# Moving the skip-and-inverse-transform stage of a fused FFN and long-convolution backward kernel from the middle of the program to its output tiles

## The chip, the cores and the metric

One core of a Trainium2 chip. The metric is the device time of one execution in microseconds (us). The kernel before took 2041.97 us (median of 6 runs, 2040.7 to 2049.8). All times below are of runs in the fast state. TensorE is called PE, VectorE DVE, ScalarE ACT, GpSimd POOL and SyncE SP, as in the profile.

## The reference, cut to what matters

The reference runs the forward pass and the gradients of one block with two branches that share a layernorm:

```python
def _f(x, ...):                         # L, D, F, N = 2048, 576, 4608, 128, bf16
    xn = _layernorm(x)
    return x + _A_ref(xn, ...) + _B_ref(xn, ...)
def _A_ref(u, ...):                     # long convolution
    K = einsum("dn,dnl,dn->dl", C, exp(dt*A*l), dt*B).real     # length-2048 kernel per channel
    y = irfft(rfft(u) * rfft(K))[:L]
    return y + u * Dskip
def _B_ref(x, Wg, Wu, Wd):              # gated FFN
    g = x @ Wg;  g = g * (g > 0)
    return (g * (x @ Wu)) @ Wd
out, vjp = jax.vjp(_f, ...);  return out, *vjp(grad_out)
```

There are thirteen outputs: the forward output, the gradient of x, eight small parameter gradients and three FFN weight gradients. Only the first two are touched by the main part of the change. Each needs a sum of three terms: the layernormed input (or the gradient) times `Dskip`, an inverse transform of the convolution, and the FFN's rows, which are accumulated over twelve chunks of F. The forward output also has x added; for the gradient of x the sum then goes through the layernorm's backward pass.

## The kernel before: the parts that matter

Two generators write the program. The FFN generator goes through 12 chunks of 384 columns; within each chunk through four groups of rows. The convolution generator is pulled beside it, so that PE always has one while the other waits. Both yield estimated us, and a pacing constant decides how much convolution is pulled per us of FFN:

```python
PACE = 0.95
W1, W2, W3 = 56.0, 400.0, 91.0
    for us in ffn.gen(ln, final):
        if us == "last": ...            # what is left of the convolution is drained here
        ft += us
        while s4_open and stt < PACE * (ft - start):
            r = next(sgen, None)
            ...
def gen(self):                          # the convolution
    ...                                 # transforms, parameters
    yield from self.p1(0)
    yield from self.both(self.p2(0, pools), 0.8 * W2, self.p1(1), W1)
    yield from self.both(self.p2(1, pools), 0.8 * W2, self.p3(0), W3)
    yield from self.p3(1)
    yield from self.grads()
```

`W3` sets how the work of `p3(0)` (products and back transforms of the first half of the 576 columns) is spread over `p2(1)` (kernel powers, second half). The end of `p3`, for each half, is the base stage:

```python
            bp = self.pool(c, f"p3_d{hf}", 2)
            for n2 in range(ST):                                   # 16 tiles of 128 rows
                S3 = self.dft(bp, self.s3_dram, n2)
                Ct = bp.tile([P, 2, 2, DH], BF16, name="bC2")
                nc.sync.dma_start(Ct[:], self.C[2][hf][:, n2])
                xt = bp.tile([P, 3, DH], BF16, name="xt")
                nc.sync.dma_start(xt[:, 0, :], g.x_v[:, n2, cols])
                nc.sync.dma_start(xt[:, 1:3, :], g.xg_dram[:, n2, :, cols])
                o = bp.tile([P, 2, DH], F32, name="base")
                v.tensor_tensor(o[:], xt[:, 1:3, :], dsk..., op=ALU.mult)              # L726
                v.tensor_tensor(o[:, 0, :], o[:, 0, :], xt[:, 0, :], op=ALU.add)
                for i in range(2):
                    v.tensor_tensor(o[:, i, :], o[:, i, :], self.back2(S3, Ct, i), op=ALU.add)
                nc.sync.dma_start(self.base_dram[:, n2, :, cols], o[:])                # L730
```

The f32 result waits in DRAM until the last FFN chunk, in which each output tile is finished once its FFN rows are complete:

```python
def final_tile(g, s4, pool, small, t):
    base = pool.tile([P, 2, D], F32, name="f_base")
    nc.sync.dma_start(base[:], s4.base_dram[:, t])
    acc = pool.tile([P, 2, D], BF16, name="f_acc")
    nc.sync.dma_start(acc[:], g.acc_dram[:, t])
    xg = pool.tile([P, 2, D], BF16, name="f_xg")
    nc.sync.dma_start(xg[:], g.xg_dram[:, t])
    ...
    nc.vector.tensor_tensor(o[:, 0, :], base[:, 0, :], acc[:, 0, :], op=ALU.add)     # L989
    ...                                                                              # layernorm backward
```

Of the kernel before, what the change touches and what calls it, by code (L numbers as in the profile page):

```python
# [14 lines left out]
P = 128  # L15
# [6 lines left out]
ST = 16  # L22
# [11 lines left out]
PACE = 0.95  # L34
W1, W2, W3 = 56.0, 400.0, 91.0
# [139 lines left out]
class Ffn:  # L175
# [121 lines left out]
    def rows(self, c, i):  # L297
        g, nc = self.g, self.g.nc
        for n in range(i, min(i + 3, 4 + NK)):
            if (c, n) not in self.R:  # L300
                t = self.dp.tile([P, ST, 144], BF16, name="rows")
                src = g.gq_dram[n] if n < 4 else g.xs_dram[n - 4]
                nc.sync.dma_start(t[:, :, 0:144 if n < 4 else min(P, D - (n - 4) * P)], src[:])
                self.R[(c, n)] = t
# [52 lines left out]
    def gen(self, ln, final):  # L357
        lu = FTC - 1
        ready = []
        for c in range(NFC):  # L360
# [10 lines left out]
            else:  # L371
# [20 lines left out]
                yield 3.0  # L392
                for ft in range(3, FTC):
# [59 lines left out]
class S4:  # L453
    def __init__(self, g, aps, outs, Dskip):
# [8 lines left out]
        self.dk_dram = two("dk_dram", [P, ST, DH])  # L463
# [3 lines left out]
        self.base_dram = d("base_dram", [P, ST, 2, D], F32)  # L467
# [177 lines left out]
    def p1(self, hf):  # L645
# [28 lines left out]
        with ExitStack() as c:  # L674
            bp = self.pool(c, f"p1_c{hf}", 3)
            for n2 in range(ST):
                S3 = self.dft(bp, self.s3_dram, n2)
                Ct = bp.tile([P, 1, 2, DH], BF16, name="bC1")
                nc.sync.dma_start(Ct[:], self.C[1][hf][:, n2])
                o = bp.tile([P, DH], BF16, name="dk_o")  # L680
                g.bal.copy(o[:], self.back2(S3, Ct, 0), DH)
                nc.sync.dma_start(self.dk_dram[hf][:, n2, :], o[:])
                yield 0.3


    def p3(self, hf):
# [26 lines left out]
        with ExitStack() as c:  # L713
            cp = self.pool(c, f"p3_c{hf}", 1)
            dsk = cp.tile([P, DH], BF16, name="dsk")
            nc.sync.dma_start(dsk[:], self.Dskip[cols].rearrange("(o d) -> o d", o=1).to_broadcast([P, DH]))
            bp = self.pool(c, f"p3_d{hf}", 2)
            for n2 in range(ST):
                S3 = self.dft(bp, self.s3_dram, n2)
                Ct = bp.tile([P, 2, 2, DH], BF16, name="bC2")  # L720
                nc.sync.dma_start(Ct[:], self.C[2][hf][:, n2])
                xt = bp.tile([P, 3, DH], BF16, name="xt")
                nc.sync.dma_start(xt[:, 0, :], g.x_v[:, n2, cols])
                nc.sync.dma_start(xt[:, 1:3, :], g.xg_dram[:, n2, :, cols])
                o = bp.tile([P, 2, DH], F32, name="base")
                v.tensor_tensor(o[:], xt[:, 1:3, :], dsk[:].unsqueeze(1).to_broadcast([P, 2, DH]), op=ALU.mult)  # L726
                v.tensor_tensor(o[:, 0, :], o[:, 0, :], xt[:, 0, :], op=ALU.add)
                for i in range(2):
                    v.tensor_tensor(o[:, i, :], o[:, i, :], self.back2(S3, Ct, i), op=ALU.add)
                nc.sync.dma_start(self.base_dram[:, n2, :, cols], o[:])  # L730
                bal.add(d=1.8)
                yield 1.8
# [16 lines left out]
    def p2(self, hf, pools):  # L749
# [4 lines left out]
        for d0 in range(hf * DH, (hf + 1) * DH, P):  # L754
# [5 lines left out]
            for s0 in range(0, dsz, SC):  # L760
# [4 lines left out]
                nc.sync.dma_start(dkr[:], self.dk_dram[hf][:, :, dd0 - hf * DH:dd0 - hf * DH + SC])  # L765
# [212 lines left out]
def final_tile(g, s4, pool, small, t):  # L978
    nc, bal = g.nc, g.bal
    inv_d = 1.0 / D  # L980
    base = pool.tile([P, 2, D], F32, name="f_base")
    nc.sync.dma_start(base[:], s4.base_dram[:, t])
    acc = pool.tile([P, 2, D], BF16, name="f_acc")
    nc.sync.dma_start(acc[:], g.acc_dram[:, t])
    xg = pool.tile([P, 2, D], BF16, name="f_xg")
    nc.sync.dma_start(xg[:], g.xg_dram[:, t])
# [19 lines left out]
def kernel(  # L1006
# [67 lines left out]
    fin = []  # L1074

    def final(t):
        if not fin:
            fin.extend(fctx.enter_context(tc.tile_pool(name=n, bufs=3, reuse_waits="tile")) for n in ("fin", "fin_small"))
        final_tile(g, s4, fin[0], fin[1], t)
# [5 lines left out]
    for us in ffn.gen(ln, final):  # L1085
        if us == "last":
            if s4_open:
                s4_open = False
                for r in sgen:
                    stt += r  # L1090
            continue
# [43 lines left out]
```

## Time and profile before

| | before |
|---|---|
| median, range (6 runs) | 2041.97 us, 2040.7 to 2049.8 |
| span of the profiled run | 2047.9 us |
| PE busy over the span | 1860.5 us, 91% |
| usual start spacings of all matmuls added up ("work") | 1700 us |
| the rest of the time from the first FFN unit ("lost") | 330 us |

The prediction shows the busy shares, the stretches and the waits. Two more lines of the page count here: what the DMA engines moved, in packets by size, and the share of their time that SyncE's queue took.

```profile
DMA packets 390368, 372.86 MB, mean 182 GB/s; under 512 B 196042, under 2 KB 314058, under 8 KB 389898
...
q1 hardware_dynamic: 339402, 288.02, 46.8%
```

Half of all packets are below 512 B. Two of the change's parts are aimed at these.

"Work" and "lost" are used throughout, as the prediction defines them (its "finer measure than busy"). The measure is stricter than PE busy: a matmul of 288 columns is recorded as 286 ns although such matmuls start 122 ns apart, so the records also cover some gaps, and 1860.5 us of busy hold 1700 us of work.

Lost time is not all waiting. The trace also records the clock granted to PE; the page's row PEclk and the column behind the busy times show it. In some short stretches it is 0.5, and there 288-column matmuls start 240 ns apart in place of 122. Its mean is 0.978 over the 2047.9 us, so at most 45 us of the lost time (an estimate from this mean) are matmuls at a slower clock.

### The profile page before, as it was taken

How to read it: one execution, taken by the hardware profiler on the slowest of the kernel's cores; microseconds unless marked ns; L12 is line 12 of the kernel's file. 1: busy time of each engine (PE TensorE's matmuls, PEld its weight loads, DVE VectorE, ACT ScalarE, POOL GpSimd, SP SyncE). 2: the span in 40 equal slices, each digit the busy share in tenths (PEclk: the TensorE clock that was granted, in tenths of full speed). 3: DMA queues.
4: the chain of work that ended last, by engine and by line, in shares of the span. 5: the costliest groups of instructions: out<-in, count | busy, mean ns of one | idle time of the engine just before them, and what ended most of it. 6: DMA issues, size and time to landing. Idle time of an engine off the chain costs nothing.

```text
span 2047.9 us, 44531 instructions
## 1 busy us (share of the span) xinstructions
PE 1860.5 (91%) x16919; PEld 1256.9 (61%) x16919; DVE 1464.3 (72%) x3633; ACT 1467.7 (72%) x3244; POOL 255.9 (12%) x321
## 2 busy tenths in 40 slices
PE   6988897989999999999999999999999889788977
PEld 3665565646756766765766766666676565456545
DVE  7454772799888787897789779779877356555573
ACT  3664673799979879888878978867878645453562
POOL 5120010001101101101101101101111100110110
PEclk8999999999999999999999999999999999999999
DMA  9556888755845748747755765687765786977797
GB/s 332 199 167 180 252 219 219 185 156 131 194 136 131 180 133 184 148 132 174 190 153 117 167 154 132 149 210 197 166 138 127 184 227 205 263 194 173 213 264 206
DMA packets 390368, 372.86 MB, mean 182 GB/s; under 512 B 196042, under 2 KB 314058, under 8 KB 389898
## 3 DMA queue, kind: packets, MB, share of 16 engines
q1 hardware_dynamic: 339402, 288.02, 46.8%
q0 software_dynamic: 29248, 63.72, 19.6%
q10 hardware_dynamic: 21504, 18.29, 3.0%
q8 instruction: 132, 2.16, 0.4%
q14 instruction: 82, 0.67, 0.1%
HBM read 220.74 MB, written 149.20 MB: 181 GB/s over the span
## 4 chain that ended last, share of the span: by engine, by line
PE 37%; ACT 23%; DVE 16%; DMA 16%; issue 5%; SPq 1%; POOL 0%; ACTq 0%; DVEq 0%; POOLq 0%
PE ps_mm L248 9%; PE ps_mm L332 8%; PE ps_mm L290 7%; ACT osx L66 3%; ACT YT L66 2%; PE ps_mm L319 2%; PE ps_s L611 2%; PE pt L272 2%; PE ps_s L869 2%; PE ps_s L612 1%; DMA base_dram<-base 1%; ACT ysn L811 1%; ACT ycs L813 1%; ACT hN L66 1%; DMA A_k<-fA 1%
## 5 line engine op out<-in xcount | busy, mean ns | idle before, releaser
L66 ACT CAST osx<-ps_mm 128x288 bf16<-128x288 f32 x716 | 279.5, 442 | 51.3 <-PE ps_mm L290 49.9
L295 POOL DMA_DIRECT2D acc_dram<-osx x176 | 152.8, 868 | 1221.5 <-ACT osx L66 865.7
L290 PE MATMUL ps_mm<-wgT,dgT 128*128 128x288 bf16 x1152 | 217.7, 288 | 4.9 <-ACT osx L66 1.5
L290 PE MATMUL ps_mm<-wuT,duT 128*128 128x288 bf16 x1152 | 215.7, 289 | 0.0
L248 PE MATMUL ps_mm<-xT,wg 128*128 128x512 bf16 x720 | 205.0, 389 | 6.5 <-ACT osx L66 3.4
L332 PEld LDWEIGHTS <-rows 128*128 128x128 bf16 x1536 | 147.7, 98 | 93.6 <-issue 4.4
L290 PE MATMUL ps_mm<-wd,hT 128*128 128x288 bf16 x1152 | 192.8, 291 | 5.1 <-ACT rg L253 1.6
L248 PE MATMUL ps_mm<-xT,wu 128*128 128x512 bf16 x720 | 194.4, 389 | 0.0
L248 PE MATMUL ps_mm<-gT,wdT 128*128 128x512 bf16 x720 | 189.5, 384 | 0.2 <-DVE upm L255 0.2
L255 DVE SCALAR_TENSOR_TENSOR upm<-rg,ps_mm 128x512 bf16<-128x512 bf16 x144 | 98.3, 683 | 113.0 <-PE ps_mm L248 75.4
L319 PE MATMUL ps_mm<-rows,hN 128*128 128x144 bf16 x2304 | 162.6, 230 | 14.9 <-DMA rows<-gq_dram 14.7
L319 PEld LDWEIGHTS <-hN 128*128 128x128 bf16 x2304 | 153.3, 100 | 18.6 <-DMA rows<-gq_dram 10.8
L66 ACT COPY YT<-ps_s 128x1024 bf16<-128x1024 bf16 x139 | 142.7, 1027 | 16.0 <-PE ps_s L869 14.8
L332 PE MATMUL ps_mm<-dgN,rows 128*128 128x384 bf16 x768 | 148.8, 329 | 2.7 <-DMA rows<-xs_dram 2.6
L885 DVE TENSOR_TENSOR pr<-X,ps_s 128x256 f32<-128x256 f32 x288 | 109.1, 415 | 51.5 <-PE ps_s L881 51.1
L66 ACT CAST dhb<-ps_mm 128x512 bf16<-128x512 f32 x144 | 86.1, 598 | 78.1 <-PE ps_mm L248 77.0
L332 PE MATMUL ps_mm<-duN,rows 128*128 128x384 bf16 x768 | 140.9, 326 | 0.0
L290 PEld LDWEIGHTS <-dgT 128*128 128x128 bf16 x1152 | 111.5, 98 | 37.0 <-issue 9.9
L290 PEld LDWEIGHTS <-hT 128*128 128x128 bf16 x1152 | 108.6, 99 | 37.8 <-issue 9.7
L290 PEld LDWEIGHTS <-duT 128*128 128x128 bf16 x1152 | 112.7, 99 | 29.7 <-issue 1.1
L248 PEld LDWEIGHTS <-wdT 128*128 128x128 bf16 x720 | 70.5, 99 | 79.7 <-issue 7.3
L248 PEld LDWEIGHTS <-wu 128*128 128x128 bf16 x720 | 70.4, 100 | 73.9 <-issue 9.5
(244 smaller groups left out, 4175.2 us busy)
## 6 DMA issues: line engine op xcount, KB each, us to landing
acc_dram<-osx POOLq DMA_DIRECT2D x192, 288.0 KB, 4.6
gT<-gT_dram SPq DMA_DIRECT2D x44, 640.0 KB, 5.9
xT<-xT_dram SPq DMA_DIRECT2D x44, 640.0 KB, 5.6
rows<-gq_dram SPq DMA_DIRECT2D x48, 576.0 KB, 4.7
rows<-xs_dram SPq DMA_DIRECT2D x48, 512.0 KB, 5.1
A_ug<-fA SPq DMA_DIRECT2D x32, 288.0 KB, 2.8
out_dram<-obw SPq DMA_DIRECT2D x96, 96.0 KB, 2.8
b_ug<-A_ug SPq DMA_DIRECT2D x32, 288.0 KB, 3.5
```

The source lines that it names most:

```text
L66: self.nc.scalar.copy(out, in_)
L248: nc.tensor.matmul(ps[:], lhsT=w[:, k, fs], rhs=rhs[:, k, :], start=(k == 0), stop=(k == NK - 1))
L255: nc.vector.scalar_tensor_tensor(upm[:], rg[:], 0.0, ps_u[:], op0=ALU.is_gt, op1=ALU.mult)
L272: nc.tensor.transpose(out=pt[:, j, :], in_=src[:, j * P:(j + 1) * P], identity=g.ident_bf[:])
L290: nc.tensor.matmul(ps[:, :DH], lhsT=lt[:, js], rhs=rh, start=(i == 0), stop=(i == len(mms) - 1))
L295: nc.gpsimd.dma_start(g.acc_dram[:, t, :, :], o[:], accum_op=ALU.add)
L319: nc.tensor.matmul(ps[:, (ft - f) * 144:(ft - f + 1) * 144], lhsT=self.hN[:, st, ft * P:(ft + 1) * P], rhs=gq[:, st, :], start=(st == 0), ...
L332: nc.tensor.matmul(ps[:, :Fc], lhsT=xs[:, st, 0:P], rhs=src[:, st, :], start=(st == 0), stop=(st == ST - 1))
L611: nc.tensor.matmul(ps[:, :DH], lhsT=CC[:], rhs=src[:, o, :], start=True, stop=False)
L612: nc.tensor.matmul(ps[:, :DH], lhsT=sm[:], rhs=src[:, other, :], start=False, stop=True)
L869: nc.tensor.transpose(out=tb[:, i * P:(i + 1) * P], in_=Y[:, ri, dl, :], identity=g.ident_bf[:])
L885: nc.vector.tensor_tensor(pr[:], X[:, dx:dx + DG, r0:r0 + 2].rearrange("p d r a -> p d (r a)").unsqueeze(2).to_broadcast(sh), psg[:, 0:DG ...
```

## The change

The intent is to spare the round trip of `base_dram` and to put the base's DVE and PE work where those engines have holes, in the last chunk. Beside this, two DMA layouts get longer runs, and the pacing constants follow the shorter convolution.

```diff
-PACE = 0.95
-W1, W2, W3 = 56.0, 400.0, 91.0
+PACE = 0.9
+W1, W2, W3 = 56.0, 400.0, 62.0
@@ rows of x and grad for the weight gradients: packed in the tile
-                nc.sync.dma_start(t[:, :, 0:144 if n < 4 else min(P, D - (n - 4) * P)], src[:])
+                w = 144 if n < 4 else min(P, D - (n - 4) * P)
+                v = t[:].rearrange("p t d -> p (t d)")[:, 0:ST * w].rearrange("p (t d) -> p t d", d=w)
+                nc.sync.dma_start(v, src[:])
@@ dk: collected in SBUF, stored once in its reader's order
-        self.dk_dram = two("dk_dram", [P, ST, DH])
+        self.dk_dram = two("dk_dram", [P, DH // SC, ST, SC])
... (the loop writes into one tile; one store behind it; the reader takes one run)
@@ the base stage leaves p3
-            for n2 in range(ST):
-                ... (the base stage above, with its store)
+    def base(self, pools, got):
+        S3, Ct, xt, xg = got
+        o = three.tile([P, 2, D], F32, name="f_base")
+        v.tensor_tensor(o[:], xg[:], dsk..., op=ALU.mult)                              # L743
+        for i in range(2):
+            for hf in range(2):
+                for ri in range(2):
+                    nc.tensor.matmul(ps, lhsT=S3[:, ri, :], rhs=Ct[:, hf, i, ri, :], ...)
+                if i == 0:
+                    nc.tensor.matmul(ps, lhsT=g.ident_bf[:], rhs=xt[:, cols], ...)     # + x
+                v.tensor_tensor(o[:, i, cols], o[:, i, cols], ps, op=ALU.add)          # L752
@@ and is made in the last chunk: fetched four tiles ahead, computed two tiles ahead
+    def final(t):
+        fetch_to(t + 4 + 1)
+        for n in range(t, min(t + 2 + 1, ST)):
+            if n not in bases:
+                bases[n] = s4.base(fin, got[n])
+        base, xg = bases[t]
+        final_tile(g, base, xg, fin[2], fin[2], t)
@@ the first three bases come early in the last chunk
+                if c == NFC - 1:
+                    yield "early"
```

More of the change, by code (lines that the diff above doesn't have):

```diff
@@ L302, in rows @@
                 src = g.gq_dram[n] if n < 4 else g.xs_dram[n - 4]
-                nc.sync.dma_start(t[:, :, 0:144 if n < 4 else min(P, D - (n - 4) * P)], src[:])
-                self.R[(c, n)] = t
+                w = 144 if n < 4 else min(P, D - (n - 4) * P)
+                v = t[:].rearrange("p t d -> p (t d)")[:, 0:ST * w].rearrange("p (t d) -> p t d", d=w)
+                nc.sync.dma_start(v, src[:])
+                self.R[(c, n)] = v
         return self.R[(c, i)]
@@ L466, in __init__ @@
         self.R_dram = d("R_dram", [P, 4, D], F32)
-        self.base_dram = d("base_dram", [P, ST, 2, D], F32)
     def pool(self, ctx, name, bufs):
@@ L675, in p1 @@
             bp = self.pool(c, f"p1_c{hf}", 3)
+            dk = self.pool(c, f"p1_d{hf}", 1).tile([P, DH // SC, ST, SC], BF16, name="dk")
+            sp = self.pool(c, f"p1_e{hf}", 2)
             for n2 in range(ST):
-                S3 = self.dft(bp, self.s3_dram, n2)
+                S3 = self.dft(sp, self.s3_dram, n2)
                 Ct = bp.tile([P, 1, 2, DH], BF16, name="bC1")
                 nc.sync.dma_start(Ct[:], self.C[1][hf][:, n2])
-                o = bp.tile([P, DH], BF16, name="dk_o")
-                g.bal.copy(o[:], self.back2(S3, Ct, 0), DH)
-                nc.sync.dma_start(self.dk_dram[hf][:, n2, :], o[:])
+                g.bal.copy(dk[:, :, n2, :], self.back2(S3, Ct, 0).rearrange("p (g d) -> p g d", d=SC), DH)
                 yield 0.3
+            nc.sync.dma_start(self.dk_dram[hf][:], dk[:])
     def p3(self, hf):
@@ L712, in p3 @@
                 yield 1.5
-        with ExitStack() as c:
-            cp = self.pool(c, f"p3_c{hf}", 1)
-            dsk = cp.tile([P, DH], BF16, name="dsk")
-            nc.sync.dma_start(dsk[:], self.Dskip[cols].rearrange("(o d) -> o d", o=1).to_broadcast([P, DH]))
-            bp = self.pool(c, f"p3_d{hf}", 2)
-            for n2 in range(ST):
-                S3 = self.dft(bp, self.s3_dram, n2)
-                Ct = bp.tile([P, 2, 2, DH], BF16, name="bC2")
-                nc.sync.dma_start(Ct[:], self.C[2][hf][:, n2])
-                xt = bp.tile([P, 3, DH], BF16, name="xt")
-                nc.sync.dma_start(xt[:, 0, :], g.x_v[:, n2, cols])
-                nc.sync.dma_start(xt[:, 1:3, :], g.xg_dram[:, n2, :, cols])
-                o = bp.tile([P, 2, DH], F32, name="base")
-                v.tensor_tensor(o[:], xt[:, 1:3, :], dsk[:].unsqueeze(1).to_broadcast([P, 2, DH]), op=ALU.mult)
-                v.tensor_tensor(o[:, 0, :], o[:, 0, :], xt[:, 0, :], op=ALU.add)
-                for i in range(2):
-                    v.tensor_tensor(o[:, i, :], o[:, i, :], self.back2(S3, Ct, i), op=ALU.add)
-                nc.sync.dma_start(self.base_dram[:, n2, :, cols], o[:])
-                bal.add(d=1.8)
-                yield 1.8
@@ new lines, in fetch @@
+    def fetch(self, pools, t):
+        g, nc = self.g, self.g.nc
+        one, ahead, three, xgp = pools
+        if t == 0:
+            self.dsk = one.tile([P, D], BF16, name="dsk")
+            nc.sync.dma_start(self.dsk[:], self.Dskip.rearrange("(o d) -> o d", o=1).to_broadcast([P, D]))
+        S3 = ahead.tile([P, 2, P], BF16, name="S3")
+        nc.sync.dma_start(S3[:], self.s3_dram[:, t])
+        Ct = ahead.tile([P, 2, 2, 2, DH], BF16, name="bC2")
+        for hf in range(2):
+            nc.sync.dma_start(Ct[:, hf], self.C[2][hf][:, t])
+        xt = ahead.tile([P, D], BF16, name="xt")
+        nc.sync.dma_start(xt[:], g.x_v[:, t, :])
+        xg = xgp.tile([P, 2, D], BF16, name="f_xg")
+        nc.sync.dma_start(xg[:], g.xg_dram[:, t])
+        return S3, Ct, xt, xg
@@ new lines, in base @@
+    def base(self, pools, got):
+        g, nc, bal = self.g, self.g.nc, self.g.bal
+        v = nc.vector
+        one, ahead, three, xgp = pools
+        S3, Ct, xt, xg = got
+        o = three.tile([P, 2, D], F32, name="f_base")
+        v.tensor_tensor(o[:], xg[:], self.dsk[:].unsqueeze(1).to_broadcast([P, 2, D]), op=ALU.mult)
+        for i in range(2):
+            for hf in range(2):
+                cols = slice(hf * DH, (hf + 1) * DH)
+                ps = self.ps()[:, :DH]
+                for ri in range(2):
+                    nc.tensor.matmul(ps, lhsT=S3[:, ri, :], rhs=Ct[:, hf, i, ri, :], start=(ri == 0), stop=(ri == 1 and i == 1))
+                if i == 0:
+                    nc.tensor.matmul(ps, lhsT=g.ident_bf[:], rhs=xt[:, cols], start=False, stop=True)
+                v.tensor_tensor(o[:, i, cols], o[:, i, cols], ps, op=ALU.add)
+        bal.add(d=2.7)
+        return o, xg
@@ L764, in p2 @@
                 dkr = parp.tile([P, ST, SC], BF16, name="dkr")
-                nc.sync.dma_start(dkr[:], self.dk_dram[hf][:, :, dd0 - hf * DH:dd0 - hf * DH + SC])
+                nc.sync.dma_start(dkr[:], self.dk_dram[hf][:, (dd0 - hf * DH) // SC])
                 dkc = parp.tile([P, SC, 2, ST], BF16, name="dkc")
@@ L974, in gen, with final_tile @@
         yield from self.grads()
-def final_tile(g, s4, pool, small, t):
+def final_tile(g, base, xg, pool, small, t):
     nc, bal = g.nc, g.bal
     inv_d = 1.0 / D
-    base = pool.tile([P, 2, D], F32, name="f_base")
-    nc.sync.dma_start(base[:], s4.base_dram[:, t])
     acc = pool.tile([P, 2, D], BF16, name="f_acc")
     nc.sync.dma_start(acc[:], g.acc_dram[:, t])
-    xg = pool.tile([P, 2, D], BF16, name="f_xg")
-    nc.sync.dma_start(xg[:], g.xg_dram[:, t])
     xn, gt = xg[:, 0, :], xg[:, 1, :]
@@ L1074, with fetch_to @@
     fin = []
-    def final(t):
-        if not fin:
-            fin.extend(fctx.enter_context(tc.tile_pool(name=n, bufs=3, reuse_waits="tile")) for n in ("fin", "fin_small"))
-        final_tile(g, s4, fin[0], fin[1], t)
+    bases = {}
+    got = {}
+    def fetch_to(n):
+        if not fin:
+            fin.extend(fctx.enter_context(tc.tile_pool(name=f"fin_{i}", bufs=n, reuse_waits="tile")) for i, n in enumerate((1, 3, 3, 6)))
+        for m in range(min(n, ST)):
+            if m not in got:
+                got[m] = s4.fetch(fin, m)
+    def final(t):
+        fetch_to(t + 4 + 1)
[4 more added lines that the diff above has]
+        final_tile(g, base, xg, fin[2], fin[2], t)
     sgen = s4.gen()
@@ L1085 @@
     for us in ffn.gen(ln, final):
-        if us == "last":
+        if us == "last" or us == "early":
             if s4_open:
@@ L1090 @@
                     stt += r
+            if us == "early":
+                fetch_to(4 + 1)
+                for n in range(3):
+                    bases[n] = s4.base(fin, got[n])
             continue
```

## The prediction

> **What bounds the kernel now.** I read the page's busy shares first, then the row of 40 slices, then a table by stretches that I cut myself, then the waits and the chain in the two worst stretches.
>
> ```profile
> PE 1860.5 (91%) x16919; PEld 1256.9 (61%) x16919; DVE 1464.3 (72%) x3633; ACT 1467.7 (72%) x3244; POOL 255.9 (12%) x321
> ...
> PE   6988897989999999999999999999999889788977
> ...
> DVE  7454772799888787897789779779877356555573
> ...
> DMA  9556888755845748747755765687765786977797
> ```
>
> TensorE is busy 91% of the span, and in the middle slices nothing is to be had from anybody else. But the last nine slices (from about 1590 us) have sevens and eights on PE while VectorE falls to five and six tenths and the DMA row climbs to nine. So the end is not bound by an engine; something there waits for transfers. The stretches (columns: us, then busy us of PE, PEld, DVE, ACT, POOL, then the granted clock, the DMA share and GB/s):
>
> ```profile
> 460.00:1322.00 862.00, 824.68 (x8172) 571.67 (x8171) 721.85 (x1721) 742.62 (x1625) 110.69 (x115) 0.99 0.64 152
> 1322.00:1484.00 162.00, 150.80 (x1488) 105.10 (x1487) 135.14 (x301) 124.94 (x261) 19.76 (x21) 0.99 0.75 192
> ...
> 1741.00:1803.00 62.00, 49.43 (x347) 31.57 (x347) 37.68 (x82) 26.86 (x60) 6.90 (x8) 0.94 0.95 262
> ...
> 1914.00:1986.00 72.00, 57.54 (x393) 35.56 (x392) 51.13 (x113) 44.92 (x103) 9.46 (x11) 0.95 0.93 249
> 1986.00:2047.90 61.90, 49.16 (x449) 36.35 (x447) 25.95 (x55) 23.86 (x54) 3.45 (x4) 0.94 0.79 217
> ```
>
> 1322 to 1484 holds the base stage of the first half of the columns (it multiplies xn and grad by Dskip, adds two back transforms and stores f32 rows), 1741 to 1803 that of the second half. There the DMA engines are 95% busy, PE only 80%. The waits in that stretch name the loads:
>
> ```profile
> DVE base L726 <- DMA xt<-xg_dram: 13.5, 9, 2.6
> PE ps_s L641 <- DMA bC<-C_ydu: 9.9, 4, 3.9
> ...
> DVE base L726 <- DMA xt<-in_A_u_dram: 5.2, 1, 5.2
> ```
>
> 1914 to 1986 is the last chunk, in which the output tiles are finished while the FFN still runs. VectorE, in order, stands before the accumulated rows, ScalarE stands behind VectorE, and PE then waits for an eviction (hN) on ScalarE:
>
> ```profile
> DVE f_o L989 <- DMA f_acc<-acc_dram: 16.0, 5, 4.6
> ACT f_acc L994 <- DVE f_base L992: 12.3, 5, 3.9
> ...
> PE pt L272 <- ACT hN L66: 9.0, 6, 3.9
> ```
>
> A finer measure than busy: the usual distance between starts of matmuls in the trace is 216, 163, 122 and 63 ns for 512, 384, 288 and 144 columns. Adding these up over the matmuls of a stretch gives its pure work; the rest of the stretch is lost. Lost share: 10% in 460 to 1322 (778 us of work in 862), 12% in 1322 to 1487 (145 in 165), 20% in 1587 to 1741, 32% in 1741 to 1803 (44.3 in 65, as its last gap reaches beyond it), 27% in 1914 to 1986 (52.4 in 72), 23% in 1986 to 2048.
>
> **What the Trainium skill says.** "TensorE: Matmul & The Clock Gate", Back-to-back issue gap: N/2.4 + 2.5 ns when warm. For 288 columns that is 122.5 ns; the trace has 122. "VectorE: DVE Perf Modes", the perf-mode tier table and the errata section: tensor_tensor with an fp32 or a PSUM operand runs at one element per cycle, (N+151)/0.96 ns. For 576 that is 757 ns; the trace has 756 (the multiply by Dskip). I use it for the one new shape, 1152 elements: 1357 ns, an estimate. "DMA: Bandwidth & Descriptors", Specifications: below 512 B a transfer is off line rate. The packets of this trace agree only in part: 256 B took 18.5 ns, 4608 B 218 ns, so small ones cost more per byte, but not wildly.
>
> **The change, part by part.**
>
> 1. The two base stages leave the middle. They hold 128 matmuls of 288 columns (15.6 us of PE) and 128 DVE instructions. Second half: 44.3 us of work less 7.8 leaves 36.5; at a lost share of 10 to 20% that needs 40 to 46 us instead of 62, so 16 to 22 us come free. First half: 145 less 7 is 138, at 10% lost 152 instead of 165, so 13 us. Together about -32.
>
> 2. base_dram goes. It was written (32 x 288 KB) and read (16 x 576 KB): 18.9 MB. xg is read once in place of twice in these stages: 4.7 MB. Total 372.9 to about 349 MB. This is mostly the cause of part 1, so I add nothing for it again.
>
> 3. The rows of xs are packed tightly in the tile, so each partition is one run of 4096 B (2048 B for the last block) and not 16 of 256 B (128 B): 122,880 packets become some 7,700. The dk tensor gets the layout of its reader: 36,864 packets of 64 B become 2,304 of 1024 B. Packets under 512 B fall from 196 thousand to about 36 thousand. The mean packet times give the DMA engines 48 us (rows) and 18 us (dk) of their time back, each. But PE waited for rows from xs only 2.6 us on its matmuls in the whole run, and the transfers are already hidden. -3.
>
> 4. dk collects in SBUF and is stored once. In 307 to 358 us (first half, where nothing else of the convolution runs) 17.8 us are lost, and the loads of C_dk stood behind stores in SyncE's order. I give it -6; the second half is hidden behind the K computation, -1. The one late store (1.1 MB, some 6 us by the kk load of the same size) may take part of this back.
>
> 5. PACE 0.95 to 0.9 and W3 91 to 62 spread the shorter work over the same FFN time; by the yields of the generators it still ends at 1266 against 1263 of 1396 virtual us. No drain at the end. 0.
>
> 6. The last chunk takes the bases over. PE: 128 matmuls, and 32 new ones that add x through the identity, 160 x 122.5 ns = 19.6 us. DVE: 16 multiplies of 1152 elements (1.36 us) and 64 adds from PSUM (0.447 us, the row of L729), 50 us. The order of instructions of the changed kernel tells where: four multiplies and about 12 adds before the second group of rows (the place of 1914 us), 8 and 34 up to the last gated activation (1986 us), the rest behind.
>  - 1866 to 1914: VectorE has room (20 of 48 us). PE pays 3.7 us. +4.
>  - 1914 to 1986: PE work 52.4 + 8 tiles x 10 x 0.1225 = 62 us. DVE busy 51.1 + 8 x 1.36 + 34 x 0.447 - 2.3 (five evictions that the order now has on ScalarE) = 75 us. That is above the stretch itself: VectorE becomes the bound. At its utilisation in the middle, 722 of 862 us or 84%, it needs 89 us; at its best slice, 96%, 78 us. I choose 85, so +13. The waits for the accumulated rows shrink, since multiplies stand before them in VectorE's order, but what VectorE gains there it spends on the bases.
>  - 1986 to the end: 4 or 5 tiles, 6 us of PE between the down-weight matmuls, with two PSUM buffers that VectorE has to free. +4.
>  Together +21.
>
> Sum: -32 - 3 - 7 + 21 = -21. From 2042: about 2020. The loads are now issued four tiles ahead, which may save more of the 19.5 us lost in 1914 to 1986 than I allowed; I put the middle at 2015.
>
> **The rivals.**
>  - A: VectorE becomes the bound of the last chunk and gives back half of the gain (my choice). For: the 75 us above. Against: nothing, except that the order could let PE run ahead. 2005 to 2025.
>  - B: The end is set by transfers alone, and removing base_dram frees it: last chunk no longer than before. For: DMA share 0.93 there, and the 16 us wait of DVE is a DMA. Against: the changed kernel fetches more per tile there, not less: C 576 KB, x 144, the transform 64, in place of 576 KB of base; and the wait is for acc, which stays. This makes 1990 to 2000, over 2%.
>  - C: With prefetches queued before it, the load of acc lands later, VectorE waits as before and the bases come on top. For: SyncE issues in order, and 1072 KB of fetches per tile go ahead of an acc of 288 KB. Against: the first five tiles are fetched before 1914. The last chunk is 40 us longer: 2035 to 2045.
>  - D: The descriptors matter more than their waits show (DMA share 0.64 in the middle falls, all landings get quicker): another -10 to -20. Against: PE loses 10% in the middle, and its waits there are for evictions, not transfers.
>
> **Range and chances.** A has most weight, B and D together a fifth, C a tenth. Predicted 2015 us, 8 in 10 between 1990 and 2036. Faster by over 2% (below 2001 us) needs B or D: 0.22. Within 2%: 0.74. Slower by over 2%: 0.04, an unforeseen stall of PE behind the two PSUM buffers.
>
> **What would show it.** Steps 1 and 2: about 349 MB, no base_dram, the time from the start of the second kernel transform (L600 with kk) to the start of the last chunk shorter by some 20 us. Step 3: some 36 thousand packets under 512 B, DMA share in the middle down from 0.64, PE busy there unchanged. Step 4: fewer than 12 us lost in the dk stage. Step 6: from the first final tile to the last gated activation, 80 to 90 us in place of 72, with VectorE over 85% busy. I am wrong if that stretch is not longer, if VectorE still has tens of us of waits for f_acc there, or if the middle (before the second base stage) shortens by more than 25 us.

## The result, and the profile after

The changed kernel took 1993.26 us (median of 8 runs, 1988.73 to 1996.18) against 2043.39 us for the kernel before (16 runs, 2039.64 to 2049.8, of the same rounds). The ratio is 0.9751, 95% interval 0.9737 to 0.9765. Ratios here and below are the mean time of one kernel's fast runs over the mean of the other's fast runs of the same rounds, so not quite the ratio of the medians. The outputs are correct. The result is inside the predicted range (1990 to 2036) but 22 us below its middle and 3 us above its lower end, and it is faster by 2.5%, an outcome that the prediction gave only 0.22.

The page of the changed kernel: busy us and instructions of each engine, then the rows of 40 slices of PE, DVE and DMA, then the packets and SyncE's queue.

```profile
PE 1842.9 (93%) x16951; PEld 1256.1 (63%) x16951; DVE 1452.8 (73%) x3593; ACT 1461.0 (73%) x3236; POOL 256.2 (13%) x321
...
PE   6989897889999999999999999999999979989988
...
DVE  7454862699878877888778878879888615664795
...
DMA  9556888656746735844854655655654577776895
...
DMA packets 214125, 348.19 MB, mean 175 GB/s; under 512 B 34266, under 2 KB 131930, under 8 KB 213402
...
q1 hardware_dynamic: 163162, 263.37, 40.6%
```

Bytes and small packets are as worked out (about 349 MB, some 36 thousand). In the row of slices the sevens of PE near the end are gone except one, and DVE now has a seven and a nine in the 38th and 39th slice: the bases. The stretches that answer to those of the prediction: the middle, the time of the old first base stage, the time of the old second one, the last chunk's gated groups, and the end.

```profile
460.00:1301.00 841.00, 807.79 (x8047) 563.85 (x8046) 691.06 (x1616) 718.04 (x1562) 111.34 (x116) 1.00 0.60 150
1301.00:1465.00 164.00, 158.45 (x1680) 114.08 (x1676) 137.56 (x325) 139.19 (x301) 19.55 (x20) 1.00 0.58 152
1745.00:1801.00 56.00, 47.52 (x460) 37.00 (x459) 37.59 (x152) 29.59 (x76) 6.93 (x8) 0.97 0.69 159
1850.00:1925.00 75.00, 68.99 (x508) 45.15 (x507) 66.68 (x141) 50.83 (x114) 10.37 (x12) 1.00 0.91 249
1925.00:1991.30 66.30, 54.82 (x474) 39.95 (x473) 41.27 (x85) 23.92 (x54) 3.45 (x4) 0.89 0.63 184
```

The reader is to compare the fourth line with the prediction's line for 1914 to 1986. The stretch is 75 us in place of 72, although PE is busy 11 us more in it and DVE 16 us more. The waits of that stretch tell why (us in total, times, longest):

```profile
DVE upm L255 <- PE ps_mm L248: 5.8, 1, 5.8
ACT f_acc L1012 <- DVE f_base L1010: 5.6, 5, 3.4
DVE f_o L1007 <- DMA f_acc<-acc_dram: 4.6, 1, 4.6
```

DVE's wait for the accumulated rows was 16.0 us and is 4.6; the wait of PE for the eviction `hN`, 9.0 us before, is no longer among the waits that matter. Multiplies and adds of the bases now stand in DVE's order where it used to wait.

Where the time went, by stretches of the FFN (wall us, with lost us in brackets; "chunk 5b" is the third group of rows of chunk 5). The old first base stage lies in the second row, the old second one in the third. "Base move" is the experiment e4 below:

| stretch | before | base move | changed | PACE 0.86 | loads ahead |
|---|---|---|---|---|---|
| first unit to chunk 5b | 923.0 (151.5) | 920.3 (150.0) | 900.6 (137.0) | 892.0 (131.3) | 922.9 (152.4) |
| chunk 5b to chunk 9 | 566.3 (63.6) | 551.7 (52.6) | 547.0 (51.5) | 540.9 (49.8) | 565.0 (62.4) |
| chunk 9 to chunk 11 | 358.7 (72.7) | 320.0 (47.2) | 335.6 (53.6) | 326.9 (39.8) | 342.1 (56.2) |
| chunk 11 to the end | 182.1 (42.1) | 191.6 (32.1) | 190.4 (30.7) | 218.4 (56.4) | 190.3 (50.4) |
| sum | 2030.1 (330) | 1983.6 (282) | 1973.6 (273) | 1978.2 (277) | 2020.3 (321) |

(Some 18 us ahead of the first unit are the same in all.) The work, wall less lost, is about 1700 us in every kernel. So all of the gain is lost time that PE no longer loses: 330 to 273 us. Up to some 13 of these 57 us are the granted clock: its mean rose from 0.978 to 0.984, which by the estimate above leaves 32 us in place of 45. No run tells whether the clock rose only because PE waited less.

The profile of the kernel before is of one of its longer runs (2049.8 us), so the table's total difference is some 6 us larger than that of the medians.

### The profile page after: what moved, and what is told of

Its sections match the earlier page's. It is cut to its first block, busy times and chain, and to the rows that moved or that the text cites. A ratio compares the mean times of both kernels' runs of the same rounds, so it can differ in the third digit from the quotient of the medians.

```text
span 1991.3 us, 44207 instructions
## 1 busy us (share of the span) xinstructions
PE 1842.9 (93%) x16951; PEld 1256.1 (63%) x16951; DVE 1452.8 (73%) x3593; ACT 1461.0 (73%) x3236; POOL 256.2 (13%) x321
## 4 chain that ended last, share of the span: by engine, by line
PE 40%; ACT 24%; DVE 19%; DMA 10%; issue 5%; SPq 0%; POOL 0%; ACTq 0%; DVEq 0%; POOLq 0%
PE ps_mm L248 10%; PE ps_mm L334 8%; PE ps_mm L290 7%; ACT osx L66 4%; PE ps_mm L321 2%; ACT YT L66 2%; PE ps_s L614 2%; ACT hN L66 2%; PE ps_s L891 2%; PE ps_s L615 2%; ACT dgN L66 1%; ACT ysn L833 1%; ACT duN L66 1%; DVE pr L907 1%; PE ps_mm L348 1%
## 5 line engine op out<-in xcount | busy, mean ns | idle before, releaser
L248 PE MATMUL ps_mm<-gT,wdT 128*128 128x512 bf16 x720 | 184.9, 379 | 0.0
```

The lines of the kernel that those rows point to most:

```text
L248: nc.tensor.matmul(ps[:], lhsT=w[:, k, fs], rhs=rhs[:, k, :], start=(k == 0), stop=(k == NK - 1))
```

## The experiments

The theory after the result: the gain is the base move, which costs little at the end because the last chunk was full of holes; the layouts give nothing; the pacing gives some, because a thinner mix of convolution and FFN loses less. The rival theory: the smaller packets relieve the DMA queues everywhere, and the base move gives only the 11 us that the prediction netted for it. Each experiment gave the reference's outputs. They ran in four sessions (e1 to e4, e5 to e8, e10 to e12, e13), each on a chip of its own and beside its own runs of the kernel before. The changed kernel was timed apart from them, so that its ratio and an experiment's are compared across sessions.

### e1_rows: the packed rows alone, in the kernel before

```diff
-                nc.sync.dma_start(t[:, :, 0:144 if n < 4 else min(P, D - (n - 4) * P)], src[:])
+                (the packed view of the change)
```

> The kernel before with the packed rows tiles alone (4096 B runs in place of 256 B). If transfers of rows were hidden as the prediction said: -3 us (ratio 0.998 to 1.000), though packets under 512 B fall by 123 thousand. If the small packets slowed everything by their use of the DMA engines (rival D): -10 us or more, ratio 0.995 or below, and the stretch of the second base stage, which was bound by transfers, gets shorter too.

Measured: 2048.16 us (22 runs) against 2046.81 (35 runs), ratio 1.0009, interval 0.9994 to 1.0025. Packets under 512 B fell from 196 thousand to 73 thousand, and the DMA share in the middle from 0.64 to 0.62. The time did not move. 123 thousand small packets fewer are worth nothing here, which fits the prediction's reading that PE waited only 2.6 us for these rows.

### e2_dk: the dk layout alone, in the kernel before

```diff
-        self.dk_dram = two("dk_dram", [P, ST, DH])
+        self.dk_dram = two("dk_dram", [P, DH // SC, ST, SC])    (with its tile, one store, one-run reads)
```

> The kernel before with the dk part alone (gathered in SBUF, one store in the layout of its reader). Prediction: -7 us, ratio 0.9965. Rival: the late single store gives it back, ratio 1.000; the profile of the whole change shows 19.8 us lost in the slice from 307 us against 17.8 before, which speaks for the rival.

Measured: 2044.37 us (14 runs), ratio 0.9989, interval 0.9971 to 1.0006. At most 6 us, with the middle of the interval at 2. In the changed kernel's slice of the dk stage (307 to 358 us) 19.8 us are lost, against 17.8 before: the stage did not get better. In that slice the waits of PE and of its weight loads for the stage's loads (`C_dk` and the transform) add up to 19.5 us in this run, against 18.6 before: they did not fall when the stores went.

### e3_all_but_pace: the changed kernel with the old pacing

```diff
-PACE = 0.9
+PACE = 0.95
```

> The changed kernel with PACE back at 0.95. Prediction (part 5: pace worth 0): the same 1993 us. Rival: at 0.95 the convolution ends at 1206 of 1396 virtual us, so almost a whole chunk runs without filler between its matmuls, which costs 10 us or more: 2003 or above.

Measured: 2006.92 us (5 runs), ratio 0.9807, interval 0.9779 to 0.9835. Against the 0.9751 of the changed kernel, PACE 0.9 is worth 0.0056 of 2045, some 11 us. Its interval does not touch that of the changed kernel. The lost time is 286 us in place of 273.

### e4_base_alone: the base move with W3 62, nothing else

```diff
(the changed kernel, with these taken back)
-PACE = 0.9
+PACE = 0.95
-                (packed rows, dk tile and layout)
+                (as in the kernel before)
```

> The changed kernel with rows and dk as before and PACE 0.95: only the bases moved into the last chunk (with W3). Prediction by its parts 1, 2 and 6: -32 + 21 = -11 us, 2031. If the move itself made the gain (last chunk only 8 us longer, as the profile shows, and 32 or more saved upstream): -24 or better, 2018 or below. If the rest (rows, dk, pace) made it: above 2030.

Measured: 2002.94 us (5 runs), ratio 0.9798, interval 0.9769 to 0.9826: some 41 us of the 51 (36 to 47 by the interval). This settles the question between the two theories. So does the comparison with e3 of the same session, which is this kernel with the two layouts added: 2006.92 us, no faster. The stretches from chunk 9 to chunk 11, cut at the starts of chunk 10, of its second group, and of chunk 11 (columns as in the prediction's table of stretches). The kernel before:

```profile
1507.00:1677.00 170.00, 155.08 (x1426) 103.97 (x1424) 100.51 (x257) 115.70 (x258) 16.30 (x18) 0.98 0.63 157
1677.00:1734.60 57.60, 57.19 (x371) 31.34 (x367) 41.02 (x128) 31.69 (x81) 0.00 (x0) 1.00 0.73 213
1734.60:1865.80 131.20, 105.73 (x860) 73.41 (x860) 72.26 (x212) 62.02 (x147) 13.83 (x16) 0.95 0.81 209
```

With the base move alone:

```profile
1489.60:1669.00 179.40, 163.68 (x1387) 106.91 (x1385) 100.97 (x289) 111.41 (x267) 13.81 (x16) 0.99 0.71 194
1669.00:1713.50 44.50, 43.45 (x297) 25.49 (x294) 25.15 (x92) 22.35 (x53) 0.00 (x0) 1.00 0.55 139
1713.50:1809.60 96.10, 88.95 (x773) 62.53 (x772) 52.66 (x168) 45.92 (x108) 14.99 (x18) 0.98 0.77 177
```

Look at the third line of each: 131.2 us with PE busy 81% become 96.1 us with PE busy 93%. The old stretch held the second base stage and then most of the parameter gradients. By the measure of lost time 36.8 us were lost there, 20.7 up to 1806 us, beside the base stage, and the rest beside the gradients; in the new third line 11.0 are. In the same run the last chunk takes 9.5 us more (182.1 to 191.6) for 19.5 us more work, because its lost time falls from 42.1 to 32.1 us.

### e5_deep: four tiles in place of two in the old second base stage

```diff
-            bp = self.pool(c, f"p3_d{hf}", 2)
+            bp = self.pool(c, f"p3_d{hf}", 2 + 2 * hf)
```

> The kernel before with four buffers in place of two in the second base stage (C, x, xg, transform and result), nothing else. If that stage lost its time to the latency of loads with too few in flight: it shortens from 62 us to about 45, ratio 0.992. If the transfers themselves are the limit there (DMA share 0.95): same time, ratio 0.998 to 1.002, and the gain of moving the bases is then that the stores to base_dram and the second reading of xg are gone.

Measured: 2046.41 us (22 runs) against 2047.99 (27 runs), ratio 0.9991, interval 0.9977 to 1.0006; the stage is as long as before. But the run tells nothing of depth. Reading the order of SyncE's instructions afterwards, it was the same as before: the loads of a tile still stood behind the store of an earlier tile, and that store waits for DVE. The additional buffers were never filled early. e13 repairs this.

### e6_w3_91: the changed kernel with the old spread of p3

```diff
-W1, W2, W3 = 56.0, 400.0, 62.0
+W1, W2, W3 = 56.0, 400.0, 91.0
```

> The changed kernel with W3 back at 91, so the transform of the first kernel half runs at its old density and ends at 965 of 1159 virtual us of the stage in place of 1080. If the even spread is part of the gain: 5 to 10 us slower than the changed kernel, 1998 to 2003. If the spread is worth nothing: 1993.

Measured: 2003.18 us (5 runs), ratio 0.9781, interval 0.976 to 0.9803. That is 0.003, some 6 us, above the changed kernel, with intervals that just overlap. Where it shows: from chunk 5b to chunk 8, where `p3(0)` runs beside `p2(1)`, 47.5 us are lost in place of 39.5. So of the 41 us of e4 about 6 belong to W3 and about 35 to the move, if the two add up.

### e7_gps: the multiply by Dskip on GpSimd

If DVE bounds the last chunk, taking 16 x 1.35 us off it should help.

```diff
-        v.tensor_tensor(o[:], xg[:], dsk..., op=ALU.mult)
+        nc.gpsimd.tensor_tensor(o[:], xg[:], dsk..., op=ALU.mult)
```

> The changed kernel with the 16 multiplies by Dskip on GpSimd in place of VectorE (22 us of VectorE less, 11 of them in the last chunk's stretch). If VectorE bounds the last chunk (the prediction's choice A): that stretch falls from 75 us to 65 to 68, total 1983 to 1986. If it is not the bound (67 of 75 us busy in the profile, 9.6 us lost by TensorE): total 1990 to 1996; if GpSimd holds up the accumulating stores it issues: slower, 2000 or more.

Measured: 2002.33 us (6 runs), ratio 0.9791, interval 0.9765 to 0.9817: about 8 us slower than the changed kernel (the intervals just touch). The profile is of its slowest run, 2014.4 us. Its groups on DVE in the last chunk (busy us and mean ns of one, then idle before):

```profile
L752 DVE TENSOR_TENSOR f_base<-f_base,ps_s 128x288 f32<-128x288 f32 x44 | 18.0, 447 | 3.0 <-PE ps_s L751 2.7 <-PE ps_s L749 0.3
L1018 DVE TENSOR_TENSOR f_o<-f_base,f_xg 128x576 bf16<-128x576 f32 x8 | 9.1, 1143 | 2.9 <-ACT f_base L1017 2.9
...
L262 DVE TENSOR_TENSOR dgT<-dhb,upm 128x512 bf16<-128x512 bf16 x8 | 7.7, 959 | 1.0 <-ACT dhb L66 1.0
L1007 DVE TENSOR_TENSOR f_o<-f_base,f_acc 128x576 bf16<-128x576 f32 x10 | 7.5, 753 | 11.3 <-DMA f_acc<-acc_dram 11.3
```

In the changed kernel the second and third of these take 754 and 419 ns; here 1143 and 959. These are means over two kinds: two of the eight L1018 took 2.30 us and two of the eight L262 2.58 and 2.59 us, and the others their usual 0.75 and 0.42. The first line, which has one input in PSUM, keeps its 446. The Trainium skill says so: "SBUF — State Buffer", Who interferes with whom: a VectorE instruction with two SBUF inputs contends with a GpSimd instruction that reads SBUF, one with at most one SBUF input and outside the two-port modes does not. This trace agrees: the slow ones all overlap a GpSimd multiply (2544 ns on average), and the L752 that lie wholly within one still take 0.44 us. The fourth line has two SBUF inputs and stayed at 753 ns; by the timeline nine of its ten lie between the multiplies, and the tenth had started before one did. And the hole that the multiplies had filled is back: DVE waits 11.3 us for the accumulated rows, against 4.6. The run therefore doesn't tell whether DVE was the bound; it shows that this relief costs more than it gives.

### e8_pace86 and e11_pace88: how far the pacing carries

```diff
-PACE = 0.9
+PACE = 0.86        (e8; 0.88 in e11)
```

> The changed kernel at PACE 0.86, so that the convolution ends at 1327 of 1396 virtual us in place of 1266, just ahead of the bases. 0.95 to 0.90 gave 11 to 14 us between the runs. If the thinner mix is what gives it: another 5 to 10 us, 1983 to 1988. If the gain was only that no chunk runs without filler: 1990 to 2000, as the gradients now run into the last chunk's loads.

> The changed kernel at PACE 0.88: the convolution ends at about 1293 of 1396 virtual us, at the start of the last chunk. At 0.86 TensorE was 22 us ahead at the last chunk and lost all of it and more there (33 us lost against 8, VectorE 92% busy). If that loss came from the gradients meeting the bases, 0.88 keeps most of the lead without the loss: ratio 0.969 to 0.973. If each step of the pace trades evenly: 0.975 to 0.977.

Measured: e8 2001.2 us (5 runs), ratio 0.9774, interval 0.9753 to 0.9794; e11 2001.51 us (5 runs; its kernel before at 2050.32), ratio 0.9759, interval 0.9731 to 0.9787. Neither beats 0.9. In e8 the last chunk starts 88 us earlier than in the kernel before, where the changed kernel gains 65, so thinner mixing does pay up to there. But gradients that didn't fit are now drained in the last chunk, just ahead of and beside the first bases. In the table above that chunk takes 218.4 us in place of 190.4. The worst 43 us of it:

```profile
1880.00:1923.00 43.00, 32.49 (x201) 20.12 (x200) 39.57 (x83) 21.18 (x47) 3.44 (x4) 0.76 0.86 244
```

DVE is busy 39.57 of 43 us, 92%, and PE only 76%. PE waits 8.8 us here for DVE's adds of the bases (L752). This is what the prediction feared of the change itself: for these 43 us DVE is close to being the bound. But it isn't shown to be the cause of the loss. Just before, while the gradients were drained (1816 to 1847), DVE was busy only 18.75 of 31 us, and in the 43 us PE's clock was 0.5 for 20.5 us, 0.76 on average.

### e10_bf16: half of the base's bytes, in the kernel before

```diff
-        self.base_dram = d("base_dram", [P, ST, 2, D], F32)
+        self.base_dram = d("base_dram", [P, ST, 2, D], BF16)
-                    v.tensor_tensor(o[:, i, :], o[:, i, :], self.back2(S3, Ct, i), op=ALU.add)
+                    v.tensor_tensor(xt[:, 1 + i, :], o[:, i, :], self.back2(S3, Ct, i), op=ALU.add)
```

> The kernel before with base_dram in bf16 in place of f32 (9.4 MB less traffic; the last add writes bf16 into the used-up xg tile, no instruction more). If the bytes of the base stage are what it waits for: the second base stage falls from 62 us to 50 to 55 and the last chunk's loads ease, -10 us, ratio 0.995. If the stage waits for the order and latency of its loads whatever their size: ratio 0.998 to 1.001. The output may differ in its last bit.

Measured: 2047.04 us (14 runs) against 2050.32 (19 runs), ratio 0.999, interval 0.9971 to 1.0009, with 9.4 MB less moved. From its first to its last multiply the second base stage took 77 us in place of 57, since the `xt` tile is now held until its store lands, and still the total stayed. The held tile is a change of its own, so the run isn't a clean test of the bytes: what they saved may have been lost to it. Shown is that half of `base_dram`'s bytes could go without any gain in the total, and that the length of a stage that runs beside the FFN is not its cost.

### e12_acc_pe: adding the accumulated rows on PE

```diff
-                    nc.tensor.matmul(ps, lhsT=g.ident_bf[:], rhs=xt[:, cols], start=False, stop=True)
-                v.tensor_tensor(o[:, i, cols], o[:, i, cols], ps, op=ALU.add)
+                    nc.tensor.matmul(ps, lhsT=g.ident_bf[:], rhs=xt[:, cols], start=False, stop=False)
+                nc.tensor.matmul(ps, lhsT=g.ident_bf[:], rhs=acc[:, i, cols], start=False, stop=True)
+                v.tensor_tensor(o[:, i, cols] if i else o0[:, cols], o[:, i, cols], ps, op=ALU.add)
@@ final_tile: its two adds of acc on DVE go
-    nc.vector.tensor_tensor(o[:, 0, :], base[:, 0, :], acc[:, 0, :], op=ALU.add)
-    nc.vector.tensor_tensor(dx, dx, acc[:, 1, :], op=ALU.add)
```

> The changed kernel with the accumulated FFN rows added on TensorE through the identity, into the same PSUM sums, so that two VectorE adds of 576 elements per tile fall away (16 x 1.5 = 24 us of VectorE, +64 matmuls or 7.8 us of TensorE); bases can then no longer run ahead of the rows. If VectorE bounds the last chunk: 5 to 10 us faster than the changed kernel, ratio 0.970 to 0.973. If the wait for the rows moves to TensorE, which stands in order before its FFN matmuls: slower, 0.978 or more.

Measured: 1991.94 us (4 runs, 1988.26 to 1992.21) against 2050.32, ratio 0.9712, interval 0.9687 to 0.9737. The changed kernel's ratio, from other rounds, is 0.9751, so this version is faster by some 0.4%, with intervals that touch: likely, not shown. It is the fastest kernel of the study. In the waits of its last chunk PE now holds the wait for the rows, and DVE waits for PE's sums:

```profile
DVE f_o L759 <- PE ps_s L758: 7.8, 5, 4.1
...
PE ps_s L758 <- DMA f_acc<-acc_dram: 4.5, 3, 3.8
```

### e13_ahead: the loads of the old base stage ahead of its stores

```diff
-            bp = self.pool(c, f"p3_d{hf}", 2)
+            depth = 2 + 2 * hf
+            bp = self.pool(c, f"p3_d{hf}", depth)
             for n2 in range(ST):
-                S3 = self.dft(bp, self.s3_dram, n2)      (and Ct, xt)
+                for m in range(n2, min(n2 + depth, ST)):
+                    if m not in got:
+                        fetch(m)                         # the same four loads
+                S3, Ct, xt = got[n2]
```

> The kernel before, with the second base stage holding four tiles in place of two and with its loads written (and so queued) up to three tiles ahead of the tile in work; in the first base stage the loads are only one tile ahead. Bytes, instructions and engine work are unchanged. It repairs the test of deeper buffers, in which the order of the issues on SyncE had not changed. Theory that the old base stage loses its time to the latency of each tile's loads (behind the store of an earlier tile in SyncE's order, and too few buffers): the second base stage takes 42 to 48 us in place of 57 and the total falls by 10 to 15 us, ratio to the kernel before 0.993 to 0.995. Theory that the stage is held by the transfer rate with what the FFN moves beside it (DMA share 0.95 to 0.97 there), or that it stands or falls with what must be done beside it and after it: stage 54 to 60 us and ratio 0.998 to 1.002.

Measured: 2040.2 us (22 runs) against 2047.76 (27 runs), ratio 0.9963, interval 0.9949 to 0.9976: some 8 us, between the two expectations. The multiply of the stage (durations min/median/max, first and last start) and the DMA traffic over the stage, before:

```profile
L726 DVE TENSOR_TENSOR base<-xt,dsk x16: 751/758/760, 1744.6 to 1801.5; 128x576 f32<-128x576 bf16 x16
```

```profile
DMA packets 15115, 16.23 MB, mean 262 GB/s; under 512 B 1239, under 2 KB 11970, under 8 KB 15110
```

With the loads ahead:

```profile
L736 DVE TENSOR_TENSOR base<-xt,dsk x16: 747/755/759, 1740.9 to 1788.2; 128x576 f32<-128x576 bf16 x16
```

```profile
DMA packets 14620, 16.25 MB, mean 307 GB/s; under 512 B 1193, under 2 KB 11613, under 8 KB 14614
```

From first to last start the stage shrinks from 56.9 to 47.3 us, and the same 16.2 MB pass at 307 GB/s in place of 262. The 95% of DMA share in the old stage was thus no limit of the transfers; too few of them were under way. The share itself went up to 1.06 (1745 to 1794 us of this run), so it doesn't end at 1. The Trainium skill, "DMA: Bandwidth & Descriptors", Rules for kernel authors, advises to issue a DMA early and wait late; this is what it is worth here. In the table, 16.6 us come free between chunk 9 and chunk 11, but 8.2 us of them are lost again in the last chunk, whose work is unchanged and whose lost time goes from 42.1 to 50.4. Why the last chunk loses more when it starts earlier is not settled: it is one profile of each. Two things in the traces fit. The parameter gradients reach 22 us into the last chunk (their last `q` starts at 1870.2 us), against 13 before, and 4.6 of the 8.2 us are lost in the chunk's first group of rows, where they run. And the granted clock was 0.5 for 23.9 us of the chunk, against 13.7 before. What the run does tell is that mending the stage in its old place gives a fifth of the 41 us that the move gives with W3.

## Why the prediction was right or wrong

The result lies in the range, near its lower end. The first half of the mechanism was as predicted: base stages that lose time in the middle, and more so the second. The second half, choice A, was not: the last chunk didn't give back half of the gain to DVE. Two of the three signs that the prediction named for being wrong came true. The stretch from the first final tile to the last gated activation did not get longer (66.1 us before, 66.7 after), and the time ahead of chunk 9 fell by 41.7 us, more than 25 (by 17.3 in e4; most of the rest is PACE). The range held by its width: three terms erred in one direction, and only the layouts, for which 10 us had been counted, in the other.

- **Part 1, first half, -13.** Right: from chunk 5b to chunk 9 the base move saves 14.6 us (566.3 to 551.7), with W3 in it.
- **Part 1, second half, -16 to -22.** Too small; e4 saves 38.7 us between chunk 9 and chunk 11. The step took the work of 65 us (44.3) and compared it with 62; with 65 its own working gives 19 to 25. And it left out the gradients behind the stage, which also lost time: 16 us of the 36.8 lost in the third line of e4's stretches. Why they lose less with the stage gone isn't shown. Of the 38.7 us, 13.2 are work that is now elsewhere (7.8 of it the base's own matmuls, the rest convolution done earlier) and 25.5 are lost time. Some 16.5 of the latter are also recovered by loads queued ahead (e13), so the waits for the stage's loads, which the prediction had read, are a large part of the cause.
- **Part 2, bytes as "mostly the cause of part 1".** Not borne out as the main cause. The bytes came out as predicted, but e13 recovers 16.5 of the 25.5 us with every byte in place, and e10 took half of `base_dram`'s away without a gain (though not cleanly). What part the bytes have in the other 9 us is open.
- **Part 3, rows -3, and part 4, dk -7.** Neither can be told from 0: the interval of e1 goes to -1 us at most, that of e2 to -6. The dk stage lost 19.8 us, not under 12. The prediction had already noted that PE hardly waited for these rows. The -7 rested on the stores that stood before the loads of `C_dk`; without them the waits for the stage's loads were no shorter (19.5 us in e2, 18.6 before).
- **Part 5, pacing 0.** Wrong. PACE is worth 11 us (e3) and W3 about 6 (e6, close to its interval). It rested on the reading that in the middle "nothing is to be had from anybody else", as PE is busy there. But from the first unit to chunk 5b the lost time falls from 151.5 to 137.0 us by mixing in less convolution. Busy PE is not working PE, which the prediction's own finer measure, 10% lost in the middle, had said. e8 and e11 show where this ends.
- **Part 6, last chunk +21.** It costs about +9: 9.5 us in e4, 8 us in the changed kernel. The step that failed is the +13 for the gated groups. From the chunk's start to the first final tile it took 3.9 us more and from the last gated activation to the end 3.6 us more, both against +4; between the two, +0.6. The two groups that were added took what was expected, 1352 ns against 1357 and 446 against 447:

```profile
L752 DVE TENSOR_TENSOR f_base<-f_base,ps_s 128x288 f32<-128x288 f32 x32 | 13.0, 446 | 0.0
L743 DVE TENSOR_TENSOR f_base<-f_xg,dsk 128x1152 f32<-128x1152 bf16 x8 | 10.8, 1352 | 0.0
```

  That is 25.1 us of durations, where the prediction had 26.1. Yet DVE is busy 66.68 us and not 75. Of the 8 us between, 1 is this, some 3.6 are other DVE instructions that no longer fall into the window, and 3.7 are overlap: the durations of the 141 instructions add up to 77.7 us, 78 ns more for each than they fill, while before, the 58.5 us of 113 filled 51.13, 65 ns more for each. The timeline (start us, us) shows such an overlap: a 0.75 us add, and the next starts 0.66 us later.

```profile
1874.97 0.75 DVE L1007 TENSOR_TENSOR f_o<-f_base,f_acc 128x576 bf16<-128x576 f32 x1
1875.63 0.75 DVE L1010 TENSOR_TENSOR f_base<-f_base,f_acc 128x576 f32<-128x576 f32 x1
```

  The step added durations to a busy time, in which overlaps count once; and with 84 to 96% as the utilisation it then made 85 us of it. 75 us at 89% were measured. So DVE did not need more than the stretch had: the bases filled the holes in which it had stood idle, and its wait for the accumulated rows fell from 16.0 to 4.6 us. PE lost 19 us between the first final tile and the last gated activation before, and 9 after. Whether DVE is close to being the bound stays open: e7 is no clean relief, e8 no clean load, and e12, which takes two of its adds per tile away, is faster by some 0.4% with intervals that touch.
- **The rivals.** B (last chunk no longer, 1990 to 2000) gave the right total, and its gated part is indeed no longer. But as a whole the chunk is 8 us longer, and most of the gain comes from ahead of it, so that the total is in part luck. C, later rows, is refuted: 16.0 us of waiting became 4.6. D, descriptors, is refuted by e1 and e2.

The sum with the measured terms, from the profiles: -15 (chunk 5b to 9, with W3), -39 (chunk 9 to 11), +9.5 (last chunk), -3 (the rest of e4), -10 (from e4 to the changed kernel, mostly PACE) = -57, the difference of the two spans (2047.9 and 1991.3). The timed runs give 50 to 51, as the profile of before was one of its longer runs.

What stays open: why the last chunk loses more when it starts earlier (e13), what the higher granted clock is due to, and how the 9 us that remain between e13 and e4 in chunks 9 and 10 divide between transfers and order.

## What to carry to other kernels

Look for places where an engine waits anyway, and try to put work in program order just ahead of that wait: here 19.5 us of additional matmul work cost 9.5 us at the end and freed far more where it came from. Before adding an operation's duration to a stretch's busy time, add up the durations that are already there and compare with that busy time, as they overlap. Where two streams are mixed by a pacing constant, re-tune it after every change of their lengths, and look at lost time, not at busy time, to see whether there is anything to win.

## What the Trainium skill lacked or had wrong

- "DMA: Bandwidth & Descriptors", Specifications, gives 512 B as the least for line rate. It doesn't say when the time of a kernel follows: here 123 thousand packets fewer below it changed the time by a ratio of 1.0009 (0.9994 to 1.0025).
- No page gives a figure for how far the DMA busy share can mislead. At a share of 0.95 the old stage moved 262 GB/s; with more loads queued the same stage moved 307, at a share of 1.06.
- "SBUF — State Buffer", Who interferes with whom, is right on VectorE and GpSimd, but gives no time for such a case: next to GpSimd multiplies of 1152 columns (2544 ns on average), two of eight 512-column bf16 multiplies took 2.58 and 2.59 us in place of 0.42.
